# A float32 first stage and TensorE transposes for the first batch of an FFT-and-MLP kernel

## The chip, the cores and the metric

The kernel runs on one core of a Trainium2 chip. The metric is the device time of one execution in microseconds (us). A core has five engines that each work through an instruction list of their own: TensorE (PE, matmuls; its weight loads are PEld), VectorE (DVE), ScalarE (ACT), GpSimd (POOL) and SyncE (SP, which here issues nearly all DMA transfers). Engines wait for one another through semaphores.

## The reference

For each of 8 batches with a sequence of 3136 rows and 256 channels:

```python
y  = irfft(rfft(x, axis=1) * F, n=3136, axis=1)      # F = filt_r + 1j*filt_i, 1569 x 256
u  = y + real(fft(fft(y, axis=1), axis=2))
un = (u - mean(u)) / sqrt(var(u) + 1e-06)            # over the 256 channels
out = u + maximum(un @ w_ch1, 0) @ w_ch2             # 256 -> 1024 -> 256
```

Everything is float32 outside; the products run in float16 on scaled values that are split into a high and a low half.

## The kernel before

**Tiling.** Each transform of length 3136 is two stages of 56-fold matmuls. For one batch, in order:

- `load_x` loads seven tiles `x` of 112x1024 (DMA issue L495) and `measure_x` takes each one's largest magnitude (L387). `weigh_x`, `pow2` and `spread` make a power of two `sx` of it: a TensorE transpose of 1 column (L364), a row maximum (L367), a broadcast (L381) and its copy (L383).
- `first` works on 14 pieces of 112x512: `x16`, the scaled high half (ACT, L533) and low half (DVE, L535); three float16 matmuls (L544); the result is split into `ast` high (ACT, L549) and low (DVE, L551) and stored to DRAM (L554).
- `load_at` loads seven tiles of 112x2048 back in the other order (L577), for batch 0 with the tables `s2`, `i1`, `i2` and `mix` between them (L582 to L591).
- `spectrum`, once per chunk (7) and channel half (2): 16 small matmuls (L618, L619), the products with the filters from PSUM (DVE, L630, L634), their combination into `yt` (POOL, or DVE for the second half of batch 0: L641, L644, L646), the split of `yt` into `y16` (ACT L653, POOL L659 or DVE L656), and a DMA transpose into `z` (L663).
- `fold` prepares the spectra for the transform over channels (`ef`, `eo`).
- `inverse1`: 14 pieces, twelve matmuls on `z` each (L732 to L734), split into `bt` (L741, L743), stored (L746). `load_b2` loads it back (L760); `inverse2` multiplies it (L779), rescales it into `ys` (L792) and stores `dy` (L803, L807).

**Groups.** The rows are then taken in 49 groups of 512: 256 rows of the first half of a sequence and the 256 that mirror them, as two `y` tiles of 128x512. `fetch` loads `y` (L825). `prepare` adds the channel transform: TensorE `mix` (L860), DVE `scaled_add` (L870), one `keep` copy for a batch's first row (ACT, L920), then statistics (L948, L949, L952 to L964). `normalize` makes `un` (L977), splits it into `u16` (L982; L985 or L988) and transposes it by DMA into `ut` (L991). `products` multiplies by the first weight (L1013) and the second (L1054), with `rectify` between them (L1041, L1043). There are 392 product steps, eight a group.

**Weights and filters.** `weight` loads raw words (L1096) and unpacks them on ACT and DVE (L1119 to L1129, L1135); `split_weights` scales and splits them (L1159 to L1163). The filters are loaded as `ft`, measured (`measure_filters`, ACT or POOL squares and DVE L429), and scaled in place by `scale_filters`.

**What sets the order.** The engines' lists are written by a planner (`Plan`). Each function above is a generator that yields an engine and an estimated duration; the planner runs them against a clock of its own, and of the tasks that stand ready for an engine it takes the one with the lowest priority number. Rings (`take`, `give`) count buffers, events (`done`, `until`) are dependences. `gate(t)` holds a task until product step t; a negative t holds nothing and only ranks. So batch 0 comes first, all of its stages have negative numbers, and the later batches are spread under the product steps:

```python
s0 = end - 1.2 - BACKED - 13 * HALF if b else -80
t0 = s0 - 4.6 - 13 * PIECE if b else -100
plan.spawn(load_x(b, t0 - 8.5 if b else -280), t0 - 8.5 if b else -280)
plan.spawn(prepare(g), 8 * g + FIRST)
```

Batch 1's `load_x` also waits until `inverse2` of batch 0 has placed a piece (`until(("placed", 0, 1))`).

## Time and profile before

| | before |
|---|---|
| median of 3 runs | 1521.86 us (1519.93 to 1523.29) |
| profiled execution | 1524.17 us |
| its span in the trace | 1522.4 us, 29999 instructions |
| mean granted TensorE clock | 0.95 |
| PE busy | 1379.6 us (91%) |
| DVE busy | 1114.9 us (73%) |
| ACT busy | 784.4 us (52%) |
| POOL busy | 541.5 us (36%) |
| DMA | 273.12 MB, mean 179 GB/s |

The profile is of one execution. Its span runs from the first instruction to the last; the execution's own time lies 1.8 us over it. A busy share is an average over all stages, so it has to be read stage by stage: with all eight batches in one span, the 91% of TensorE say little of the first 200 us. PEclk is the clock that TensorE was granted, as a share of 2.4 GHz. In the rows, a tile's name stands without its number, `out<-in`.

### The profile page before, as it was taken

Reading aid. Unit: us, or ns where it says so; the run is one execution under the profiler, and the core shown is the slowest. Engines: PE = TensorE matmul, PEld = TensorE weight load, DVE = VectorE, ACT = ScalarE, POOL = GpSimd, SP = SyncE. Lnnn points to the kernel's source line nnn. Section 1 sums busy time; section 2 is a strip of 40 time slices with the busy share of each in tenths; the row PEclk is TensorE's granted clock in tenths of the full one; section 3 lists DMA queues with packets and bytes.
Section 4 is the critical chain, followed back from the end, with each engine's and each line's share of the span. In section 5 each row is a group of like instructions: output and inputs, shape, how many; then the busy total and the mean of one; then the engine's idle time right before and its main releaser. Section 6 shows DMA issues by size and latency. Waiting matters only on the chain.

```text
span 1522.4 us, 29999 instructions
## 1 busy us (share of the span) xinstructions
PE 1379.6 (91%) x11217; PEld 935.0 (61%) x11217; DVE 1114.9 (73%) x2409; ACT 784.4 (52%) x1450; POOL 541.5 (36%) x675
## 2 busy tenths in 40 slices
PE   3442599999999999999999999999999999999998
PEld 1341257765776567666666666666666677666666
DVE  6774977787787877888688867878778878465563
ACT  4543565455464655565555545465455646443442
POOL 4461046501671038400860057211760167210100
PEclk9555589999999999999999999999999999999999
DMA  7999497956988698948987599758997698735521
GB/s 214 207 211 220 126 197 165 241 144 175 220 189 198 170 211 172 263 123 197 226 178 213 144 214 214 218 138 192 210 196 197 163 218 181 179 83 124 132 68 43
DMA packets 419827, 273.12 MB, mean 179 GB/s; under 512 B 234048, under 2 KB 361072, under 8 KB 419680
## 3 DMA queue, kind: packets, MB, share of 16 engines
q1 hardware_dynamic: 419680, 271.19, 77.0%
q8 instruction: 88, 1.44, 0.4%
q14 instruction: 59, 0.48, 0.1%
HBM read 113.31 MB, written 102.76 MB: 142 GB/s over the span
## 4 chain that ended last, share of the span: by engine, by line
PE 56%; DVE 4%; DMA 2%; issue 2%; ACT 1%; SPq 1%; POOL 1%; ACTq 0%; POOLq 0%; DVEq 0%
PE acc L1054 23%; PE h L1013 23%; PE y L779 3%; PE s L544 2%; PE mix L860 2%; DVE y L870 1%; PE i L732 1%; PE i L734 1%; PE i L733 1%; DMA ut<-u 1%; PE s L618 1%; PE s L619 1%; DMA b<-d 1%; DVE st L948 1%; DVE h L1043 1%
## 5 line engine op out<-in xcount | busy, mean ns | idle before, releaser
L1054 PE MATMUL acc<-w2s,h 128*128 128x256 f16 x4704 | 591.9, 273 | 2.8 <-DVE y L1068 2.7
L1013 PE MATMUL h<-ut,w1s 128*128 128x512 f16 x2352 | 578.0, 382 | 16.1 <-DMA ut<-u 11.6
L1054 PEld LDWEIGHTS <-h 128*128 128x128 f16 x4704 | 452.0, 98 | 142.3 <-issue 18.8
L1041 ACT ACTIVATE h<-h 128x512 f16<-128x512 f32 x392 | 233.5, 596 | 482.7 <-PE h L1013 481.9
L1043 DVE SCALAR_TENSOR_TENSOR h<-h,h 128x512 f16<-128x512 f32 x392 | 268.3, 684 | 213.9 <-ACT h L1041 213.1
L1013 PEld LDWEIGHTS <-w1s 128*128 128x128 f16 x2352 | 228.4, 98 | 222.9 <-issue 19.6
L988 POOL TENSOR_TENSOR u<-un,u 128x512 f16<-128x512 f32 x94 | 109.6, 1167 | 598.4 <-ACT u L982 524.6
L870 DVE SCALAR_TENSOR_TENSOR y<-mix,alpha,y 128x508 f32<-128x508 f32 (+1 forms) x368 | 160.5, 475 | 38.6 <-PE mix L860 33.4
L544 PE MATMUL s<-x,s 112*112 112x512 f16 x336 | 100.3, 425 | 20.6 <-ACT x L533 9.7
L644 POOL TENSOR_TENSOR yt<-yt,t 128x224 f32<-128x224 f32 x105 | 70.2, 668 | 134.3 <-DVE yt L636 83.4
L977 ACT ACTIVATE un<-y,sb 128x256 f32<-128x256 f32 x196 | 110.7, 595 | 12.5 <-DVE sb L964 8.5
L659 POOL TENSOR_TENSOR y<-yt,y 128x448 f16<-128x448 f32 x105 | 109.6, 1048 | 18.7 <-ACT y L653 15.4
L630 DVE TENSOR_TENSOR yt<-s,ft 128x448 f32<-128x448 f32 x112 | 69.1, 617 | 32.2 <-PE s L619 29.3
L535 DVE SCALAR_TENSOR_TENSOR x<-x,sx,x 112x512 f16<-112x512 f32 x111 | 86.9, 808 | 6.4 <-ACT x L533 6.3
L732 PE MATMUL i<-z,i 112*112 112x256 f16 x224 | 65.5, 292 | 25.2 <-DMA z<-y 20.1
L551 DVE TENSOR_TENSOR ast<-s,ast 112x512 f16<-112x512 f32 x112 | 74.5, 684 | 15.3 <-ACT ast L549 14.9
L711 POOL TENSOR_TENSOR eo<-ef,eo 128x448 f16<-128x448 f32 (+6 forms) x62 | 59.7, 966 | 71.8 <-ACT eo L708 71.6
L387 DVE TENSOR_REDUCE mx<-x 112x1 f32<-112x1024 f32 x56 | 67.5, 1211 | 23.6 <-DMA x<-x 23.6
L743 DVE TENSOR_TENSOR bt<-i,bt 112x512 f16<-112x512 f32 x112 | 74.8, 684 | 13.6 <-ACT bt L741 13.3
L948 DVE BATCH_NORM_STATS2 st<-y 128x6 f32<-128x256 f32 x196 | 80.8, 412 | 3.0
L792 ACT ACTIVATE ys<-y,alpha 128x512 f32<-128x512 f32 x112 | 73.4, 685 | 18.2 <-PE y L779 18.0
L544 PEld LDWEIGHTS <-s 112*112 112x112 f16 x336 | 46.3, 143 | 56.6 <-issue 37.1
(130 smaller groups left out, 1609.8 us busy)
## 6 DMA issues: line engine op xcount, KB each, us to landing
x<-x SPq DMA_DIRECT2D x56, 448.0 KB
d<-ast SPq DMA_DIRECT2D x112, 224.0 KB
at<-d SPq DMA_DIRECT2D x56, 448.0 KB
d<-bt SPq DMA_DIRECT2D x112, 224.0 KB
b<-d SPq DMA_DIRECT2D x56, 448.0 KB
out<-y SPq DMA_DIRECT2D x98, 256.0 KB
y<-dy SPq DMA_DIRECT2D x92, 256.0 KB
dy<-ys SPq DMA_DIRECT2D x96, 224.0 KB
```

Of the source, the lines that this page charges most:

```text
L535: nc.vector.scalar_tensor_tensor(x16[:, 1], x, sx[:112, 1:2], x16[:, 0], op0=ALU.mult, op1=ALU.subtract)
L544: nc.tensor.matmul(p, s1[:, hs], x16[:, hx], start=i == 0, stop=i == 2)
L659: nc.gpsimd.tensor_tensor(y16[:, :, 1, :112], ytv, y16[:, :, 0, :112], op=ALU.subtract)
L732: nc.tensor.matmul(p[:, i], i1[:, j + i, 0], z[:, i, 0], start=True, stop=False)
L870: nc.vector.scalar_tensor_tensor(out, p, al, y, op0=ALU.mult, op1=ALU.add)
L948: nc.vector.bn_stats(st[:, 2 * t + k], y[:, t, k])
L977: nc.scalar.activation(un[:, k], y[:, t, k], AF.Identity, bias=sb[:, i, 1:2], scale=sb[:, i, 3:4])
L988: nc.gpsimd.tensor_tensor(u16[:, :, :, 1], unv, u16[:, :, :, 0], op=ALU.subtract)
L1013: nc.tensor.matmul(p.rearrange("p (t k q) -> p t k q", t=2, k=2), w1s[:, d, hw, 128 * f : 128 * f + 128], utv[:, :, :, d, hx], start=i == ...
L1041: nc.scalar.activation(h[:, 0], p, AF.Relu)
L1043: nc.vector.scalar_tensor_tensor(h[:, 1], p, 0.0, h[:, 0], op0=ALU.max, op1=ALU.subtract)
L1054: nc.tensor.matmul(acc[:, kind], h[:, hh, c0 : c0 + 128], w2s[:, f, hw], start=f == 0 and kind == 0 and i == 0, stop=f == 7 and kind == 1 ...
```

## The change

Line numbers of the changed kernel are its own.

1. **First stage of batches 0 and 1** (`WIDE = 2`): one float32 matmul per piece on x as it was loaded (L534), with the table `s1f` in float32. The scale `sx` is applied in the eviction (ACT L551, DVE L556), so `x16` falls away. In batch 0 the pieces use four `psf` and two `pso` banks, and `ast` is also kept in buffers of `un`, `u16` and `h`; the first six pieces are multiplied before `sx` is known.
2. **Filters unscaled.** `scale_filters` goes. `conjugate` turns the sign of part of `ft`, and the scale `pF` is a scalar of the filter product (`filtered`, L654), in all batches. Six of the eight filter squares are ACT's, four were.
3. **Batch 0's spectra transposed on TensorE.** `yt` is laid out as [128, 2, 448]; four float32 transposes per chunk and half (L680) go into a `psh` bank, and ACT (L685) and DVE (L687) split that into `z`. The 14 DMA transposes of batch 0 and its `y16` go. Its spectra use the `pso` banks.
4. **Loads.** Tables are issued by `load_tables`, the first two of `s2` ahead of the stores' end. Batch 1's x no longer waits for `placed` and is ranked ahead of batch 0's second inverse. All weights are loaded early, four of them into `w1s` and `w2s` themselves.
5. **Group 0 ahead.** Its channel mixing runs when the last spectrum of batch 0 is done, in `pso` banks; each half has its own `weigh` and is spawned to `normalize` by itself. The first two `b2` and `inverse2` are ranked at -60.

```diff
     def first(b, q, t):
-        yield until(("sx", b), *((("s1",),) if b == 0 else ()))
+        yield until(*((("sx", b), ("s1",)) if b >= WIDE else (("s1f",), ("x", b, q // 2))))
...
+        elif b or q > 5:
+            yield until(("sx", b))
+        kp = yield take(ring)
...
+        if wide:
+            yield "PE", 0.86 if b else 1.2
+            nc.tensor.matmul(p, s1f, x, start=True, stop=True)
...
+            yield until(("sx", b))
...
         yield "ACT", 0.53
-        nc.scalar.copy(st[:, :, 0], p)
+        if wide:
+            nc.scalar.activation(st[:, :, 0], p, AF.Copy, scale=sx[:112, 1:2])
...
         yield "DVE", 0.64
-        nc.vector.tensor_tensor(st[:, :, 1], p, st[:, :, 0], op=ALU.subtract)
+        if wide:
+            nc.vector.scalar_tensor_tensor(st[:, :, 1], p, sx[:112, 1:2], st[:, :, 0], op0=ALU.mult, op1=ALU.subtract)
...
     def load_x(b, t):
-        if b == 1:
-            yield until(("placed", 0, 1))
...
     def spectrum(b, ch, hf, t):
+        def filtered(out, p, f):
+            nc.vector.scalar_tensor_tensor(out, p, pF[:, 1:2], f, op0=ALU.mult, op1=ALU.mult)
+        filtered(t1, p, fr)
...
+        filtered(t2, p, fi)
...
+        if b == 0:
+            kp = yield take("psh")
+            pt = spare(f"yT_{ch}_{hf}")[:112].rearrange("p (j c) -> p j c", j=4)
+            yield "PE", 1.2
+            for j in range(4):
+                nc.tensor.transpose(pt[:, j], yt[:, hf, 112 * j : 112 * j + 112], ident)
...
+            yield "ACT", 0.53
+            nc.scalar.copy(z[:, :, 0], pt)
+            yield "DVE", 0.64
+            nc.vector.tensor_tensor(z[:, :, 1], pt, z[:, :, 0], op=ALU.subtract)
+            give("psh", kp)
...
     def prepare(g):
+        if g == 0:
+            yield until(("spectrum", 0, 6, 0), ("spectrum", 0, 6, 1))
+            kp, pm = yield from mixing()
         yield until(("y", g))
...
+            if g == 0:
+                yield from weigh(slice(2 * t, 2 * t + 2))
+                plan.spawn(normalize(g, t, y, sb, ut), -56 + t)
...
     def weight(i):
-        at = RAW_AFTER[i]
-        yield until(("d1", 0, at) if at < 14 else ("spectrum", 0, (at - 14) // 2, at % 2))
+        yield until(("at", 0, min(i, 6)))
...
-        yield until(*((("weight", i - 1),) if i else ()))
...
-        end = brought(b, 0) - 4
-        s0 = end - 1.2 - BACKED - 13 * HALF if b else -80
-        t0 = s0 - 4.6 - 13 * PIECE if b else -100
-        plan.spawn(load_x(b, t0 - 8.5 if b else -280), t0 - 8.5 if b else -280)
+        x0, t0, s0, piece, half = ((-280, -100, -80, PIECE, HALF), (-30, -7, 9, 0.9, 1.25))[b] if b < 2 else (0,) * 5
...
+        plan.spawn(load_x(b, x0), x0)
...
-        plan.spawn(fetch(g), 8 * g + FIRST - 3)
-        plan.spawn(prepare(g), 8 * g + FIRST)
+        plan.spawn(fetch(g), 8 * g + FIRST - 3 if g else -56)
+        plan.spawn(prepare(g), 8 * g + FIRST if g else -55)
```

The first place is VectorE's list in batch 0's first stage, from the copy of the scale `sx` on. Before:

```order
L383 COPY sx_0_157<-pb_x0_163 128x2
L535 SCALAR_TENSOR_TENSOR x16_0_0_169<-x_0_0_117,sx_0_157,x16_0_0_169 112x512
L535 SCALAR_TENSOR_TENSOR x16_0_1_170<-x_0_0_117,sx_0_157,x16_0_1_170 112x512
L429 TENSOR_REDUCE mF_112<-squares_1_158 128x1
L551 TENSOR_TENSOR ast_0_0_193<-s1_0_0_179,ast_0_0_193 112x2x256
L551 TENSOR_TENSOR ast_0_1_199<-s1_0_1_189,ast_0_1_199 112x2x256
L535 SCALAR_TENSOR_TENSOR x16_0_3_192<-x_0_1_120,sx_0_157,x16_0_3_192 112x512
L429 TENSOR_REDUCE mF_112<-squares_2_166 128x1
L535 SCALAR_TENSOR_TENSOR x16_0_4_198<-x_0_2_121,sx_0_157,x16_0_4_198 112x512
```

After:

```order
L386 COPY sx_0_174<-pb_x0_177 128x2
L556 SCALAR_TENSOR_TENSOR ast_0_0_183<-s1_0_0_134,sx_0_174,ast_0_0_183 112x2x256
L556 SCALAR_TENSOR_TENSOR ast_0_1_184<-s1_0_1_135,sx_0_174,ast_0_1_184 112x2x256
L556 SCALAR_TENSOR_TENSOR ast_0_2_185<-s1_0_2_139,sx_0_174,ast_0_2_185 112x2x256
L556 SCALAR_TENSOR_TENSOR ast_0_3_186<-s1_0_3_140,sx_0_174,ast_0_3_186 112x2x256
```

The splits of `x16` are gone, the evictions `ast` follow one another from the scale on (five more rows like these come next), and the first filter reduction stands behind the ninth of them.

The second place is SP's list while batch 0's spectra are made, from the load of `at_0_4` on. Before:

```order
L577 DMA at_0_4_305<-d1_0_168 112x8x256
L582 DMA s2_82<-c_s2 112x896
L585 DMA i1_83<-c_i1 112x896
L663 DMA_TRANSPOSE z_0_0_445<-y16_1_105 128x8x128
L663 DMA_TRANSPOSE z_0_0_445<-y16_0_104 128x8x128
L577 DMA at_0_5_330<-d1_0_168 112x8x256
L582 DMA s2_82<-c_s2 112x896
L585 DMA i1_83<-c_i1 112x896
L663 DMA_TRANSPOSE z_0_1_493<-y16_2_106 128x8x128
L577 DMA at_0_6_366<-d1_0_168 112x8x256
L582 DMA s2_82<-c_s2 112x896
```

After:

```order
L589 DMA at_0_4_246<-d1_0_133 112x8x256
L596 DMA s2_83<-c_s2 112x896
L600 DMA i1_84<-c_i1 112x896
L596 DMA s2_83<-c_s2 112x896
L600 DMA i1_84<-c_i1 112x896
L596 DMA s2_83<-c_s2 112x896
L600 DMA i1_84<-c_i1 112x896
L603 DMA i2_85<-c_i2 112x512
L605 DMA mix_86<-c_mix 128x640
L1165 DMA w1s_93<-w1 128x1024
L589 DMA at_0_5_262<-d1_0_133 112x8x256
L1165 DMA w1s_93<-w1 128x1024
L589 DMA at_0_6_277<-d1_0_133 112x8x256
```

The transposes into `z` no longer stand between the loads; the tables stand in one run, and two raw weights follow them.

The third place is SP's list around group 0's `y`, from the last stores of `dy` ahead of `b2_0_3` on. Before:

```order
L803 DMA dy_0_1091<-ys_0_1_1074 56x4x256 x2
L760 DMA b2_0_3_1094<-d2_0_116 112x8x256
L495 DMA x_1_0_895<-x 112x1024
L1096 DMA raw_5_1136<-w2 128x1024
L495 DMA x_1_1_896<-x 112x1024
L495 DMA x_1_2_897<-x 112x1024
L495 DMA x_1_3_921<-x 112x1024
L495 DMA x_1_4_956<-x 112x1024
L495 DMA x_1_5_994<-x 112x1024
L825 DMA y_0_118<-dy_0_1091 128x512 x2
L495 DMA x_1_6_1025<-x 112x1024
```

After, from the store of a `bt` in chunk 5 on:

```order
L784 DMA d2_0_116<-bt_0_5_1_971 112x1024
L487 DMA x_1_5_970<-x 112x1024
L487 DMA x_1_6_1041<-x 112x1024
L784 DMA d2_0_116<-bt_0_6_0_1030 112x1024
L784 DMA d2_0_116<-bt_0_6_1_1042 112x1024
L798 DMA b2_0_0_1063<-d2_0_116 112x8x256
L798 DMA b2_0_1_1069<-d2_0_116 112x8x256
L798 DMA b2_0_2_1104<-d2_0_116 112x8x256
L841 DMA dy_0_1119<-ys_0_0_1086 56x3x256
```

The loads of batch 1's x and the raw weights, which stood between the `dy` stores and `y_0`, now stand among the stores of `bt`, ahead of the first load of `b2` (the other tiles of x and the weights further up). After the row `b2_0_3`, `y_0` is next:

```order
L841 DMA dy_0_1119<-ys_0_1_1112 56x4x256
L845 DMA dy_0_1119<-ys_0_0_1086 28x256
L841 DMA dy_0_1119<-ys_0_1_1112 56x4x256
L845 DMA dy_0_1119<-ys_0_0_1086 28x256
L798 DMA b2_0_3_1131<-d2_0_116 112x8x256
L863 DMA y_0_119<-dy_0_1119 128x512 x2
L841 DMA dy_0_1119<-ys_0_2_1157 56x4x256 x2
```

Nothing of batch 1 is left between the `dy` stores and `y_0`.

## Rows read from the trace of the kernel before

**Rows 1.** Busy time by stage: us, then each engine (x instructions), PEclk, DMA share, GB/s
```profile
0.00:20.00 20.00, 0.93 (x3) 0.74 (x4) 9.71 (x15) 2.49 (x5) 2.99 (x12) 1.00 0.92 260
20.00:55.20 35.20, 18.16 (x45) 7.88 (x44) 26.36 (x48) 24.05 (x47) 15.64 (x17) 0.85 0.57 176
55.20:115.00 59.80, 27.84 (x308) 25.43 (x308) 46.83 (x79) 27.58 (x56) 41.56 (x49) 0.56 1.01 214
115.00:152.00 37.00, 8.70 (x55) 4.46 (x55) 16.44 (x26) 13.26 (x24) 4.78 (x4) 0.55 0.91 222
152.00:179.00 27.00, 11.21 (x37) 5.36 (x37) 23.95 (x66) 10.81 (x21) 0.00 (x0) 0.50 0.42 127
179.00:202.60 23.60, 19.98 (x65) 9.00 (x66) 19.52 (x42) 22.23 (x42) 3.46 (x3) 0.64 0.50 144
202.60:1522.40 1319.80, 1292.82 (x10706) 882.13 (x10703) 972.10 (x2136) 684.02 (x1257) 473.09 (x591) 1.00 0.78 177
```

**Rows 2.** Timeline, first stage: start us, us, engine line op, tiles, [idle before <-releaser]
```profile
19.75 0.16 DVE L383 COPY sx<-pb_x 128x2 f32<-128x2 f32 x1 [0.68 <-PE pb_x L381]
...
42.09 0.42 PE L364 MATMUL pt_F<-ident,mF 128*1 128x128 f32 x1
...
48.04 0.68 DVE L551 TENSOR_TENSOR ast<-s,ast 112x512 f16<-112x512 f32 x1
...
51.01 0.32 SPq L577 DMA_DIRECT2D at<-d  x1
...
55.28 0.23 PE L618 MATMUL s<-s,at 112*128 112x56 f16 x1 [8.64 <-DMA at<-d]
```

**Rows 3.** Groups by line and shape, VectorE, 0 to 204 us: busy us, mean ns | idle before
```profile
L535 DVE SCALAR_TENSOR_TENSOR x<-x,sx,x 112x512 f16<-112x512 f32 x27 | 24.3, 918 | 2.0 <-ACT x L533 2.0
L551 DVE TENSOR_TENSOR ast<-s,ast 112x512 f16<-112x512 f32 x28 | 18.6, 685 | 4.3 <-ACT ast L549 4.0
L387 DVE TENSOR_REDUCE mx<-x 112x1 f32<-112x1024 f32 x14 | 17.1, 1220 | 19.4 <-DMA x<-x 19.4
L1121 DVE SCALAR_TENSOR_TENSOR w<-raw,cv 128x512 int32<-128x512 int32 x8 | 6.2, 781 | 0.2
```

**Rows 4.** Groups by line and shape, VectorE, 55 to 115 us
```profile
L743 DVE TENSOR_TENSOR bt<-i,bt 112x512 f16<-112x512 f32 x14 | 9.3, 683 | 3.4 <-ACT bt L741 3.4
...
L630 DVE TENSOR_TENSOR yt<-s,ft 128x448 f32<-128x448 f32 x14 | 8.6, 616 | 5.2 <-PE s L619 4.9
...
L656 DVE TENSOR_TENSOR y<-yt,y 128x448 f16<-128x448 f32 x7 | 5.4, 773 | 0.7 <-ACT y L653 0.7
```

**Rows 5.** Waits, 0 to 240 us: engine line waited for: us, times, longest us
```profile
PE i L732 <- DMA z<-y: 18.3, 3, 7.8
```

**Rows 6.** Timeline, second inverse to dense work, 112 to 206 us
```profile
114.21 0.69 DVE L743 TENSOR_TENSOR bt<-i,bt 112x512 f16<-112x512 f32 x1 [0.59 <-ACT bt L741]
...
123.78 1.92 PE L779 MATMUL y<-b,i 112*64 112x256 f16 x12 [10.27 <-DMA b<-d]
...
133.48 2.59 SPq L495 DMA_DIRECT2D x<-x  x5
...
152.04 0.40 ACT L920 COPY keep<-y 1x256 f32<-1x256 f32 x1 [4.42 <-DMA y<-dy]
...
155.65 1.66 DVE L870 SCALAR_TENSOR_TENSOR y<-mix,alpha,y 128x508 f32<-128x508 f32 x3
...
175.28 0.66 DVE L985 TENSOR_TENSOR u<-un,u 128x512 f16<-128x512 f32 x1
...
179.06 5.30 PE L1013 MATMUL h<-ut,w1s 128*128 128x512 f16 x12 [3.59 <-DMA ut<-u]
...
202.65 2.50 PE L1013 MATMUL h<-ut,w1s 128*128 128x512 f16 x6
```

**Rows 7.** Page, costliest groups of the whole span: busy us, mean ns | idle before
```profile
L1041 ACT ACTIVATE h<-h 128x512 f16<-128x512 f32 x392 | 233.5, 596 | 482.7 <-PE h L1013 481.9
...
L1043 DVE SCALAR_TENSOR_TENSOR h<-h,h 128x512 f16<-128x512 f32 x392 | 268.3, 684 | 213.9 <-ACT h L1041 213.1
```

More of the change, by code (lines that the diff above doesn't have):

```diff
@@ L31 @@
 LAG = 2
+WIDE = 2
 YBUFS = 5
@@ L106, in until, with set @@
         self.post(t, self.resume, task, None)
-    def set(self, event):
-        event.time = self.end
+    def set(self, event, now=False):
+        event.time = self.now if now else self.end
         for task, events in event.waiting:
@@ L537, in first @@
             )
[L538 to L547 removed]
+            if q % 2:
+                give("big", 21 * b + q // 2)
+        elif b or q > 5:
+            yield until(("sx", b))
@@ L904, in prepare, with mixing @@
         yield until(*(("eo", b, c) for b, c in pieces(g, 224)), *((("i2",),) if g == 0 else ()))
+        tiles = [(256 * g + 128 * t, 256 * g + 128 * t + 128) for t in range(2)]
+        ring = "psf" if g else "pso"
+        def mixing():
+            kp = yield take(ring)
+            pm = bank(f"mix_{g}") if g else ps_o.tile([128, 512], F32, tag="pso", name="mix_0")
+            pm = pm.rearrange("p (t c) -> p t c", t=2)
+            for t, (g0, g1) in enumerate(tiles):
+                r0 = g0 % RING
+                yield "PE", 0.4
+                channels(pm[:, t], lambda e, h: eo[:, e, h, r0 : r0 + 128], t == 0, t == 1)
+            mixed[0] = 256 * g + 256
+            done("mixed", g)
+            return kp, pm
+        if g == 0:
+            yield until(("spectrum", 0, 6, 0), ("spectrum", 0, 6, 1))
+            kp, pm = yield from mixing()
         yield until(("y", g))
-        tiles = [(256 * g + 128 * t, 256 * g + 128 * t + 128) for t in range(2)]
         y = ys_of.pop(g)
@@ L921, in prepare, with weigh @@
                     nc.scalar.copy(keep[row, 1], pn)
-                    give("psf", kn)
+                    give(ring, kn)
                     fix = t, row, keep, alphas[b], ku
-        kp = yield take("psf")
-        pm = bank(f"mix_{g}").rearrange("p (t c) -> p t c", t=2)
-        for t, (g0, g1) in enumerate(tiles):
-            r0 = g0 % RING
-            yield "PE", 0.4
-            channels(pm[:, t], lambda e, h: eo[:, e, h, r0 : r0 + 128], t == 0, t == 1)
-        mixed[0] = 256 * g + 256
-        done("mixed", g)
+        if g:
+            kp, pm = yield from mixing()
         mv = tp.tile([128, 4, 2], F32, tag="mv", name=f"mv_{g}")
         st = tp.tile([128, 4, 6], F32, tag="st", name=f"st_{g}")
+        sb = tp.tile([128, 4, 4], F32, tag="sb", name=f"sb_{g}")
+        def weigh(part):
+            yield "ACT", 0.25
+            nc.scalar.activation(sb[:, part, 0], mv[:, part, 1], AF.Sqrt, bias=eps)
+            mu, v = mv[:, part, 0], mv[:, part, 1]
+            r, q, c, s = (sb[:, part, i] for i in range(4))
+            yield "DVE", 0.25
+            nc.vector.reciprocal(r, r)
+            yield "DVE", 0.25
+            nc.vector.scalar_tensor_tensor(q, r, -8.0, r, op0=ALU.mult, op1=ALU.mult)
+            yield "DVE", 0.25
+            nc.vector.scalar_tensor_tensor(c, v, EPS, q, op0=ALU.add, op1=ALU.mult)
+            yield "DVE", 0.25
+            nc.vector.scalar_tensor_tensor(s, c, 24.0, r, op0=ALU.add, op1=ALU.mult)
+            yield "DVE", 0.25
+            nc.vector.scalar_tensor_tensor(q, mu, -1.0, s, op0=ALU.mult, op1=ALU.mult)
+        if g == 0:
+            kt = yield take("ut")
+            ut = mp.tile([128, 2, 8, 128], F16, tag="ut", name=f"ut_{g}", bufs=2)
+            ready[g] = y, ut, kt
         for t, (g0, g1) in enumerate(tiles):
@@ L1097, in weight @@
             done("raw", i)
-            yield until(("raw", i))
+            yield until(("raw", i), *((("weight", i - 2),) if i > 1 else ()))
         ws, m = raws[name]
```

298 lines of the change are left out of this document (155 added, 143 removed).

## The prediction

> **What bounds the kernel now.** I read the busy time by stage first [rows 1]. From 202.6 us to the end TensorE is busy 1292.8 of 1319.8 us at the full clock: nothing but its own work counts there. The 202.6 us ahead of it are different: TensorE is busy 86.8 us of them (the sum of the first six rows), mostly at the lower of its two clock levels (1.2 GHz). This stretch is a chain through one batch, and the kernel ends earlier by what that chain loses. The other batches run under the products, so an edit to them counts only as TensorE time.
>
> The timeline gives the joints of the chain. The scale of x is there at 19.9 us, the last split of the first stage is done at 48.7, the first spectrum starts at 55.3 [rows 2]. The last `bt` is split by 114.9, second inverse matmuls start at 123.8, the first `y` row is touched at 152.0, mixed rows are added from 155.7, and group 0's first product starts at 179.1; dense work starts at 202.65 [rows 6].
>
> The sum is made against the profiled execution, 1524.2 us; the median of the runs is 2.3 us lower, and I take the difference off at the end.
>
> **First stage (0 to 55.3).** Removed: per piece one ACT scaling and one DVE split of 0.92 us [rows 3]; the three float16 matmuls become one float32 matmul on x as loaded, which waits only for x and a PSUM bank. Six banks are open before the scale is known, so six of 14 pieces are multiplied in the idle time ahead of 19.9, and eight remain. No row has a float32 matmul of 512 columns. The nearest is the float32 transpose of 128 columns, 0.42 us [rows 2], so 1.67 us for 512. From above: a matmul that is issued as two such halves, 3.34 us. From below it is free, and VectorE's eviction sets the pace: 14 x 0.69 [rows 3]. I take 1.67, the only row of that type and engine at the same low level: the first bank is free at 21.2 (19.9, then an ACT pass of 0.6 as [rows 7] and a split of 0.69), 8 x 1.67 = 13.4, the last eviction another 1.3: 35.9. (Below: 19.9 + 0.6 + 9.6 = 30.1. Above: 21.2 + 26.7 + 1.3 = 49.2, no gain.) The way from the last split to the first spectrum took 6.6 us; two table loads of 196 KB now lie ahead of it, 1.5 us at the 260 GB/s of the first 20 us to 1.8 at the 214 of the next stage [rows 1], partly beside the last stores; I add 1.0: spectra start at 43.5, **11.8 us** earlier. Filter measuring moves to ACT, six squares instead of four; it ends before the spectra, and its cover is the matmuls' pace: without it, two squares.
>
> **Spectra to the last `bt` (59.6 us now).** The 14 transposing transfers go, and the wait for them: TensorE waited 18.3 us for z [rows 5]. But VectorE is busy 46.8 of 59.8 us and the DMA queues are full, share 1.01 [rows 1].
> - VectorE: the filter product gets a scalar. A three-operand form over 512 PSUM elements takes 684 ns [rows 7], 1.34 ns each; the two-operand form over 448 took 616 [rows 4], 1.38: nothing. Off: seven splits `y` of 0.77 (5.4). Added: 14 splits of the transposed tile, priced as `bt`, 0.68 each (9.6) [rows 4]. Two more weights are unpacked here, four operations of 0.78 at most each [rows 3], 5.8 with the short one, and one maximum of x 1.2. Sum 58.0.
> - ACT loses the filter scaling, and 14 casts of `z` replace 14 of `y`: busy 27.6 of 59.8 us [rows 1], not counted.
> - TensorE: 27.8 us busy now, plus 56 transposes of 0.42 = 23.5: 51.3.
> - DMA, from tile shapes: spectra inputs 3.2 MB, tables 2.9, weights 4.2, `bt` 3.2 and, new here, batch 1's x 3.2: 16.7 MB. At 214 GB/s from about 38 us that ends at 116, with x and the weights at the 260 of the first 20 us [rows 1] at 110.
>
> So three engines each need about what the stage takes today, and I expect no gain in it: `bt` done at 103, second inverse at 114 instead of 123.8 (the 8.9 us between them stay, and 2 for the DMA backlog). Bounds 104 (TensorE's 51.3 alone, then 8.9) and 120 (116 and one load of 4.3, as long as the first input took from its issue [rows 2]).
>
> **`y` of group 0.** It took 28.3 us from the second inverse to its landing, because batch 1's x was issued ahead of it on SP's queue, from 133.5 on [rows 6]. The change puts those loads, and the weights, before the second inverse: six x tiles and one weight, 3.3 MB at 222 GB/s [rows 1] = 14.6 us. Landing at 114 + 13.7 = 127.7. VectorE, which now has six maxima (1.22 [rows 3], 7.3 in all) and four weights (2.9 each, 11.6) between the last `bt` and this add, is free at 103 + 7.3 + 11.6 + about 3 for three scale chains = 125, just ahead. One copy of `keep` later, at 128.5, the add starts (155.7 now).
>
> **Add to first product** took 23.4 us (155.65 to 179.06), with VectorE busy 23.95 of 27 us [rows 1, 6]. The channel mixing is now done ahead and each half normalises by itself, but VectorE's order still puts both halves, two evictions of batch 1 and part of group 1 before the second half's split, so I leave 23.4: first product at 151.9, **27 us** earlier.
>
> **First product to dense work.** Until 202.65 TensorE waited for the second weight matrix. By then three first-product steps, one second-product step and an inverse were done, about 6 us of work at the full clock (half of the 0.44 us that 512 columns took at the lower level [rows 6]): as good as dense from 196.7 with batch 1's first stage done. After: the weights are split before group 0, so dense from 151.9, but six of batch 1's pieces, for which there is no idle time left (0.84 us each at the full clock, half of 1.67), and some 1.5 us of low clock come on top: 158.4. Gain **38.3**.
>
> **Behind that** nothing of the 1319.8 us goes: the filter product's new form and the new tile layout are VectorE, ACT and GpSimd work under TensorE. That cover is 348 us wide for VectorE (972 of 1320 busy). I take 1 us for batch 1's tighter chain and its float32 matmuls. 1524.2 - 37.3 = 1486.9, against the median **1485 us**.
>
> **Rivals.**
> *Less: TensorE sets the spectra's pace.* Its 51.3 us are at the low level. If it still stands in line for the transposes' inputs as it now does for z, 51.3 + 18.3 = 69.6, 10 us over 59.6: 1495; with the float32 matmul at its upper bound instead, 13 more than forecast, 1498; both, 1508. For it: the granted clock was 0.56 in that stage, and the products of one chunk now stand behind another's transposes on one queue. Against: the transposes wait for the same engines as the products do, so their waits may fall into one.
> The Trainium skill, "TensorE: Matmul & The Clock Gate", Part 4 (PE-mode transpose), says that a transpose does not count as busy for the clock. By that rule the added 23.5 us would lift nothing and this rival is the likelier; here 0.56 was granted without any of them, so the trace cannot yet say.
> *More.* The queue waits vanish with the transposing transfers and the bounds from below hold: second inverse at 104 and first stage at 30.1, 10 + 6 us less: 1469. For it: VectorE's rows in that stage are swollen (splits 773 against the 683 of a larger one). Against: the full DMA queues.
> *Slower: batch 1 starves the products.* Ten of its 14 first-stage stores now fall into the dense stretch, 2.3 MB on top of about 20.7 (106 us at 195 GB/s, my estimate between the rows' 177 and 214), before batch 0's groups run out. At the 127 GB/s of 152 to 179 the 23 MB take 181 us, 75 over: 1560. It decides below 23 MB / (106 + 37 us) = 161 GB/s. Against: 127 was a stretch with the queues half idle (0.42), and under demand they moved 214 to 222.
> *No change*: the weights or batch 1's maxima hold group 0 back until 179 after all. VectorE has 22 us of work there, not 52.
>
> **Numbers.** Forecast 0.58 (1475 to 1494), less 0.17, more 0.19, slower 0.04, no change 0.02. The first three are faster: 0.94. A difference of 0.2%, 3 us, is about what a measurement of this kernel can tell. The range leaves out the slower end and the edges: 1464 to 1508; it takes in the bounds of the first stage (-6, +13) and of the second inverse (-10, +6), which need not fall together.
>
> **What would show it.** First spectrum near 43.5 us, with float32 matmuls of 1.7 us; `bt` ending near 103; no x load between `dy` and `y`; first add near 128; first product near 152, and TensorE dense from there. I am wrong if the dense stretch, from its first product on, shows waits on DMA of more than a few us, if the transposes take far from 0.42 us, or if the first product comes later than 165.

## The result and the profile after

The changed kernel takes 1481.88 us (median) against 1522.57 us: a ratio of 0.972, 95% interval 0.968 to 0.976. It was timed a second time beside the last experiments: 1483.14 us, ratio 0.9752 (0.9738 to 0.9765). The forecast was 1485, the range 1464 to 1508. One of the changed kernel's first four runs took 2082.58 us, at a granted clock of 0.648, and is not in the ratios.

| | before | after |
|---|---|---|
| median of 4 runs | 1522.57 us | 1481.88 us |
| profiled execution, its span | 1524.17, 1522.4 us | 1478.77, 1477.0 us |
| mean granted TensorE clock | 0.95 | 0.966 |
| PE busy | 1379.6 us | 1379.7 us |
| DVE, ACT, POOL busy | 1114.9, 784.4, 541.5 us | 1109.6, 763.7, 528.5 us |
| DMA | 273.12 MB | 269.48 MB |

The median before has one run more than the three ahead of the prediction, 1528.86 us. TensorE is busy for the same 1380 us. What went is its idle time, 142.8 us before and 97.3 after. First the busy time by stage, with the stages cut at nearly the same joints as in [rows 1] (118.0 is the first add and not the touch of `y` 0.6 us before it; the last two lines are the product stretch, cut once more at 165 us):

```profile
0.00:18.30 18.30, 8.40 (x15) 3.33 (x15) 9.67 (x15) 3.94 (x7) 1.28 (x10) 0.95 0.91 277
18.30:39.10 20.80, 9.34 (x19) 3.69 (x19) 11.76 (x29) 12.84 (x27) 6.96 (x10) 0.75 0.91 291
39.10:97.40 58.30, 36.66 (x380) 32.51 (x380) 53.75 (x96) 24.28 (x46) 38.00 (x42) 0.70 0.92 261
97.40:118.00 20.60, 8.32 (x40) 4.43 (x41) 19.19 (x47) 13.66 (x29) 3.72 (x3) 0.50 0.67 187
118.00:142.00 24.00, 14.80 (x43) 5.48 (x41) 22.95 (x63) 16.45 (x30) 6.73 (x6) 0.64 0.39 106
142.00:165.00 23.00, 23.00 (x138) 12.89 (x137) 13.86 (x25) 11.65 (x20) 0.00 (x0) 0.98 0.67 181
165.00:1477.00 1312.00, 1279.19 (x10615) 872.08 (x10613) 978.43 (x2122) 680.85 (x1251) 471.84 (x590) 0.99 0.73 177
```

The six lines up to 165 us answer to the first six of [rows 1]: 165 us in place of 202.6, with more product work done in them. In the spectra's stage, from 39.1 to 97.4 us, VectorE is busy 53.8 us for 46.8, TensorE 36.7 for 27.8, and the DMA queues moved 261 GB/s where they moved 214. TensorE's granted clock is 0.70 there, it was 0.56.

The joints of the chain, from the timeline:

```profile
18.19 0.16 DVE L386 COPY sx<-pb_x 128x2 f32<-128x2 f32 x1 [0.68 <-PE pb_x L384]
...
20.11 8.70 PE L534 MATMUL s<-x,s1f 112*112 112x512 f32 x16 [1.95 <-DVE ast L556]
...
31.07 0.75 DVE L556 SCALAR_TENSOR_TENSOR ast<-s,sx,ast 112x512 f16<-112x512 f32 x1 [0.42 <-ACT ast L551]
...
39.16 0.23 PE L635 MATMUL s<-s,at 112*128 112x56 f16 x1 [5.49 <-DMA at<-d]
...
43.64 1.94 PE L680 MATMUL yT<-ident,yt 128*112 128x128 f32 x8
...
96.78 0.68 DVE L781 TENSOR_TENSOR bt<-i,bt 112x512 f16<-112x512 f32 x1
...
104.19 3.62 PE L817 MATMUL y<-b,i 112*64 112x256 f16 x20 [1.29 <-DMA b<-d]
...
117.42 0.40 ACT L981 COPY keep<-y 1x256 f32<-1x256 f32 x1
...
117.97 1.79 DVE L912 SCALAR_TENSOR_TENSOR y<-mix,alpha,y 128x508 f32<-128x508 f32 x4
...
140.90 3.69 PE L1080 MATMUL h<-ut,w1s 128*128 128x512 f16 x12
...
148.60 0.82 PE L1121 MATMUL acc<-w2s,h 128*128 128x256 f16 x6
```

Against [rows 2] and [rows 6]: the scale of x comes 1.6 us earlier, the last split of the first stage ends at 31.8 us for 48.7, the first spectrum starts at 39.2 for 55.3, the last split of `bt` at 96.8 for 114.2, the second inverse at 104.2 for 123.8, `y` is touched at 117.4 for 152.0, the first add at 118.0 for 155.7, the first product at 140.9 for 179.1. The second product now follows 7.7 us behind the first; it stood at 200.1 before.

Behind that there is something new. The two longest waits of the product stretch, from the timeline of TensorE:

```profile
316.78 3.73 PE L543 MATMUL s<-x,s 112*112 112x512 f16 x8 [8.41 <-DVE x L522]
...
818.48 2.58 PE L543 MATMUL s<-x,s 112*112 112x512 f16 x5 [5.62 <-DVE x L522]
```

TensorE stood 8.4 us at 308 us and 5.6 us at 813, at two seams between batches. The kernel before had no wait over 2.8 us behind 202.6 us. Both came again in the second profile of the changed kernel, 8.38 and 5.61 us: they are in the lists, not in the run.

### The profile page after: what moved, and what is told of

Same layout as the page of the kernel before. It is cut to its first block, busy times and chain, and to the rows that moved or that the text cites. A ratio compares the mean times of both kernels' runs of the same rounds, so it can differ in the third digit from the quotient of the medians.

```text
span 1477.0 us, 29967 instructions
## 1 busy us (share of the span) xinstructions
PE 1379.7 (93%) x11245; PEld 934.4 (63%) x11245; DVE 1109.6 (75%) x2391; ACT 763.7 (52%) x1407; POOL 528.5 (36%) x660
## 2 busy tenths in 40 slices
DMA packets 405297, 269.48 MB, mean 182 GB/s; under 512 B 219408, under 2 KB 346656, under 8 KB 405152
## 4 chain that ended last, share of the span: by engine, by line
PE 50%; DVE 6%; DMA 1%; ACT 1%; issue 0%; POOL 0%; SPq 0%; ACTq 0%; DVEq 0%
PE acc L1121 20%; PE h L1080 20%; PE y L817 2%; DVE y L912 2%; PE s L543 2%; PE mix L902 1%; DVE h L1110 1%; DVE st L1025 1%; PE i L770 1%; DMA ut<-u 1%; PE s L635 1%; PE i L772 1%; PE i L771 1%; PE s L636 1%; DVE y L1135 1%
## 5 line engine op out<-in xcount | busy, mean ns | idle before, releaser
L1080 PEld LDWEIGHTS <-w1s 128*128 128x128 f16 x2352 | 227.9, 98 | 210.5 <-issue 12.7
L668 POOL TENSOR_TENSOR yt<-yt,t 128x224 f32<-128x224 f32 x98 | 64.5, 658 | 159.9 <-DVE t L654 157.0
L697 POOL TENSOR_TENSOR y<-yt,y 128x448 f16<-128x448 f32 x98 | 100.7, 1034 | 7.5 <-ACT y L695 7.0
L654 DVE SCALAR_TENSOR_TENSOR yt<-s,pF,ft 128x448 f32<-128x448 f32 x98 | 66.4, 677 | 31.2 <-PE s L636 29.2
L654 DVE SCALAR_TENSOR_TENSOR t<-s,pF,ft 128x448 f32<-128x448 f32 x126 | 84.1, 674 | 6.6 <-PE s L636 6.6
L779 ACT CAST bt<-i 112x512 f16<-112x512 f32 x112 | 65.2, 586 | 33.9 <-PE i L772 26.0
L543 PE MATMUL s<-x,s 112*112 112x512 f16 x252 | 67.4, 392 | 16.1 <-DVE x L522 14.8
L830 ACT ACTIVATE ys<-y,alpha 128x512 f32<-128x512 f32 x112 | 73.5, 685 | 11.9 <-PE y L817 11.6
L1135 DVE SCALAR_TENSOR_TENSOR y<-acc,beta,y 128x512 f32<-128x512 f32 x98 | 70.5, 742 | 11.8 <-PE acc L1121 11.3
L390 DVE TENSOR_REDUCE mx<-x 112x1 f32<-112x1024 f32 x56 | 67.0, 1209 | 10.1 <-DMA x<-x 10.1
L720 POOL TENSOR_TENSOR ef<-yt 128x224 f32<-128x224 f32 x112 | 72.9, 671 | 0.8 <-DVE yt L665 0.4
```

Of the source, the lines that this page charges most:

```text
L543: nc.tensor.matmul(p, s1[:, hs], x16[:, hx], start=i == 0, stop=i == 2)
L654: nc.vector.scalar_tensor_tensor(out, p, pF[:, 1:2], f, op0=ALU.mult, op1=ALU.mult)
L697: nc.gpsimd.tensor_tensor(y16v[:, 1], yh, y16v[:, 0], op=ALU.subtract)
L1080: nc.tensor.matmul(p.rearrange("p (t k q) -> p t k q", t=2, k=2), w1s[:, d, hw, 128 * f : 128 * f + 128], utv[:, :, :, d, hx], start=i == ...
L1135: nc.vector.scalar_tensor_tensor(y[:, t], acc, beta, y[:, t], op0=ALU.mult, op1=ALU.add)
```

## Experiments

Twelve runs followed, one of them of the changed kernel itself (after_again). The table gives the joints of each profiled execution in us from the span's start (the last `bt` is the start of its split). "Rest" is the span less the start of the first second-product. The two executions of the changed kernel differ by 1.4 to 2.6 us at every joint from the scale of x on (18.2 and 19.9), so a head's difference under 2.5 us says nothing. "Against changed" is against the mean of its two medians, 1482.5. The kernel before took 1519.17 to 1522.57 us beside the several groups of runs, and the changed one lay 40.7 and 37.1 us under it, so under 4 us that column says nothing by itself. The ratios given below are to the kernel before, beside the run.

| kernel | median | against changed | first spectrum | last `bt` | second inverse | first add | first product | first second-product | rest |
|---|---|---|---|---|---|---|---|---|---|
| before | 1522.57 | +40.1 | 55.3 | 114.2 | 123.8 | 155.7 | 179.1 | 200.1 | 1322.3 |
| changed | 1481.88 | | 39.2 | 96.8 | 104.2 | 118.0 | 140.9 | 148.6 | 1328.4 |
| after_again | 1483.14 | | 41.4 | 98.3 | 105.6 | 119.5 | 143.0 | 151.2 | 1329.3 |
| dma_transposes | 1496.01 | +13.5 | 40.5 | 101.6 | 120.6 | 136.8 | 154.8 | 164.1 | 1332.8 |
| narrow | 1498.26 | +15.8 | 52.1 | 108.7 | 115.9 | 131.8 | 155.1 | 163.2 | 1334.4 |
| group0_plain | 1493.30 | +10.8 | 39.9 | 97.0 | 104.7 | 126.1 | 143.5 | 152.6 | 1339.8 |
| weights_late | 1500.82 | +18.3 | 43.2 | 97.7 | 107.5 | 130.2 | 148.1 | 167.8 | 1331.0 |
| before_x1_free | 1519.00 | +36.5 | 55.8 | 112.2 | 125.3 | 147.7 | 168.8 | 194.1 | 1322.7 |
| twice_pe | 1489.59 | +7.1 | 40.2 | 102.9 | 111.1 | 128.7 | 147.3 | 156.5 | 1330.2 |
| twice_dve | 1487.13 | +4.6 | 41.7 | 97.9 | 106.2 | 123.1 | 144.7 | 154.5 | 1331.1 |
| wide1 | 1487.22 | +4.7 | 40.4 | 97.1 | 104.5 | 120.2 | 143.5 | 152.0 | 1331.7 |
| b1_sooner | 1478.69 | -3.8 | 41.0 | 98.0 | 105.5 | 119.4 | 143.2 | 150.1 | 1327.8 |
| b1_denser | 1489.07 | +6.6 | 42.6 | 99.7 | 107.1 | 120.9 | 144.7 | 151.6 | 1334.7 |
| come16_sooner | 1466.65 | -15.9 | 39.9 | 97.0 | 104.5 | 118.4 | 142.1 | 149.8 | 1315.0 |

Every kernel has three first-product steps behind it when the rest begins. "before" and "before_x1_free" also have the whole of batch 1's first stage behind them, the changed kernel ten of its 14 pieces, so the rest of these two is not to be compared with the others: four pieces at 0.86 us are 3.4 us.

### One part undone at a time

**dma_transposes.** In `spectrum`, with the low half of `y16` on VectorE again for the second channel half of batch 0:

```diff
-        if b == 0:
+        if b < 0:
             kp = yield take("psh")
...
-        yield "POOL", 1.03
-        nc.gpsimd.tensor_tensor(y16v[:, 1], yh, y16v[:, 0], op=ALU.subtract)
+        if b == 0 and hf == 1:
+            yield "DVE", 0.55
+            nc.vector.tensor_tensor(y16v[:, 1], yh, y16v[:, 0], op=ALU.subtract)
...
```

> The changed kernel with batch 0's spectra transposed by DMA again (14 transposing transfers, y16 split), all else as changed. My theory, from the prediction's sum (three engines each need what the stage takes, so the transposes alone exchange one cost for another): within 4 us of the changed kernel's 1481, that is 1477 to 1485, and the stretch from the first spectrum to the last split of bt stays near the 58.2 us of the changed kernel. Rival (the wait for z set that stage, and TensorE's transposes removed it): 10 to 18 us slower, 1491 to 1499, the stretch 68 us or longer, with TensorE waiting for z on DMA again.

Measured: 1496.01 us, ratio 0.9834 (0.9809 to 0.9860). The rival had the time right, 13.5 us, and mostly the wrong place. TensorE does wait for `z` on DMA again, 13.7 us in four waits, but the stage grew by less: 61.1 us from the first spectrum to the start of the last `bt` split for 57.6. Most of the loss stands behind it: 19.0 us from there to the second inverse, 7.4 in the changed kernel. Busy time by stage of that stretch, SP's issues in it, and TensorE's first second-inverse matmul:

```profile
97.00:121.00 24.00, 5.03 (x22) 4.04 (x24) 21.32 (x42) 11.31 (x24) 2.31 (x2) 0.50 1.03 289
...
102.81 4.94 SPq L487 DMA_DIRECT2D x<-x  x5
...
110.21 0.93 SPq L802 DMA_DIRECT2D b<-d  x2
...
120.64 3.62 PE L821 MATMUL y<-b,i 112*64 112x256 f16 x20 [2.26 <-DMA b<-d]
```

The DMA queues are full (1.03) and move 289 GB/s: five loads of batch 1's x are now issued behind the last split of `bt`, and weights shortly ahead of it, all in front of the loads of `b2`; in the changed kernel the last x was issued by 94.8 us, ahead of that split. The same stretch of the changed kernel is short and its queues are not full (0.62):

```profile
97.40:104.20 6.80, 0.38 (x3) 0.12 (x3) 6.63 (x13) 3.07 (x9) 0.00 (x0) 0.50 0.62 173
```

So the transposes on TensorE paid, and less by the wait for z of [rows 5] than by the loads that are now early. With the transposing transfers the queues moved 203 GB/s at a share of 1.24 between 60 and 70 us, without them 363 at 1.07. Whether this queue time or the transposes' places in SP's list held the loads back is not separated.

**narrow.**

```diff
-WIDE = 2
+WIDE = 0
...
-        yield "SP", 0.3, -60
+        yield "SP", 0.3, -300
         nc.sync.dma_start(s1, a["c_s1"])
```

> The changed kernel with WIDE = 0: the first stage of batches 0 and 1 in three float16 matmuls on scaled and split x again, its table loaded first; all else as changed. My theory (the float32 first stage brought the first spectrum forward by most of the 16.1 us between 55.3 and 39.2, and the chain behind it passes that on whole): first spectrum at 50 to 54, time 11 to 15 us over the changed kernel's 1481: 1492 to 1496. Rival (the chain behind absorbs it, since weights and batch 1's maxima hold group 0 anyway): less than 5 us slower.

Measured: 1498.26 us, ratio 0.9847 (0.9823 to 0.9871), first spectrum at 52.1 us. This is my theory, with a time 2.3 us over its range: the 11.8 us that the first spectrum lost against the mean of 40.3 are still there at the first product (13.2). Nothing behind it took them up.

**group0_plain.** `prepare(0)` takes the path of every other group, at its old ranks:

```diff
...
-        plan.spawn(fetch(g), 8 * g + FIRST - 3 if g else -56)
-        plan.spawn(prepare(g), 8 * g + FIRST if g else -55)
+        plan.spawn(fetch(g), 8 * g + FIRST - 3)
+        plan.spawn(prepare(g), 8 * g + FIRST)
```

> The changed kernel with group 0 prepared as every other group (mixing after y has come, one chain for both halves, its old ranks). My theory (the prediction left 23.4 us from add to first product, and the trace after shows 22.9, so preparing ahead gives little): within 4 us of the changed kernel's 1481. Rival (it is what keeps the 22.9 from growing, because batch 1's evictions would come in between): 8 us or more slower.

Measured: 1493.30 us, ratio 0.9817 (0.9795 to 0.9838). My theory misses. The rival has the time (10.8 us), but not its reason. The first add comes 7.4 us later, but the first product only 1.6 and the first second-product 2.7 us later than the mean of the changed kernel's two. So the 22.9 us from add to product did not grow; they shrank to 17.5. The rest, where the edit changes no work, is 10.9 us longer. TensorE's busy time behind 160 us says where, here and in the second execution of the changed kernel:

```profile
160.00:1492.40 1332.40, 1295.67 (x10685) 882.07 (x10683) 991.39 (x2135) 683.97 (x1255) 471.93 (x590) 0.99 0.73 175
```

```profile
160.00:1480.50 1320.50, 1286.74 (x10675) 877.15 (x10672) 983.28 (x2134) 682.79 (x1254) 471.30 (x590) 0.99 0.74 177
```

TensorE is idle 36.7 us here and 33.8 there, and busy 1295.7 for 1286.7 us with nearly the same instructions. Of these 9 us about 5 are a lower clock behind more, shorter waits (my estimate from the granted clock in steps of 10 us: eight steps lie under 0.97, four in after_again). An edit in the head gives the planner another order for everything behind it, and that order is worth some us by itself.

**weights_late.** The weights at their old places and buffers, one after another:

```diff
-RAW_IN = (None, None, "ys", "ys", "ut", "ut", None, None)
+RAW_IN = ("ys", "ys", "b2", "ut", "ut", "ys", "b2", "ys")
+RAW_AFTER = (6, 7, 8, 9, 10, 17, 18, 15)
...
-            yield until(("raw", i), *((("weight", i - 2),) if i > 1 else ()))
+            yield until(("raw", i))
```

> The changed kernel with the weights loaded and unpacked one after another at their old places (as in the kernel before). My theory (the early weights are what lets the second product follow the first: 11 us of the prediction's sum, and what kept the early x alone from paying in the kernel before): first product within 5 us of 140.9, first second-product 15 us or more after it, time 10 to 16 us over the changed kernel's 1481: 1491 to 1497. Rival (VectorE has room for them): under 4 us slower.

Measured: 1500.82 us, ratio 0.9870 (0.9833 to 0.9908): 18.3 us, more than I expected, and the largest of the four. The first product and the first second-product on TensorE:

```profile
148.08 5.30 PE L1081 MATMUL h<-ut,w1s 128*128 128x512 f16 x12 [21.31 <-DMA ut<-u]
...
167.76 0.37 PE L1122 MATMUL acc<-w2s,h 128*128 128x256 f16 x1 [1.65 <-ACT w2s L1234]
```

The second product stands 19.7 us behind the first, as the theory has it (21 us before, 7.7 changed); the first product is also 6 us late, which the theory did not have. The four parts undone cost 58.4 us together, more than the whole change gained, so their prices cannot be added.

**before_x1_free.** The kernel before with

```diff
-        if b == 1:
-            yield until(("placed", 0, 1))
```

> The kernel before with one thing changed: batch 1's x no longer waits until a piece of the second inverse is placed, so its loads stand among the stores of bt and not ahead of group 0's y. My theory (those loads held y back by 14.6 us): from the first second-inverse matmul to the first touch of y 14 to 17 us instead of 28.3; first product 9 to 15 us earlier than 179.1; time 1508 to 1514 against 1522.6. Rival (the second weight matrix and VectorE's list hold the products anyway): under 4 us faster.

Measured: 1519.00 us against 1520.73 for the kernel before, ratio 0.9980 (0.9962 to 0.9998): the rival. Half of the mechanism was right: from the second inverse to the first touch of `y` it took 19.6 us for 28.3, and the first product came 10.2 us earlier. But TensorE's next row is the end of that gain:

```profile
168.84 4.15 PE L1011 MATMUL h<-ut,w1s 128*128 128x512 f16 x12
...
194.10 0.37 PE L1052 MATMUL acc<-w2s,h 128*128 128x256 f16 x1 [1.65 <-ACT w2s L1159]
```

The second product waits for the second weight matrix until 194.1 us, 6.0 earlier than before. Early x alone is worth 0.2%; with the weights early beside it, taking those away costs 18.3 us. Weights early without x was not run.

### What sets the spectra's stage

**twice_pe.** Each transpose twice (`for j in (0, 1, 2, 3, 0, 1, 2, 3)`).

> The changed kernel with each of the 56 transposes of batch 0 made twice into the same bank: 56 x 0.24 = 13.4 us more of TensorE between the first spectrum and the last split of bt, nothing more for any other engine. My theory (VectorE, busy 53.8 of 58.3 us there, sets that stage): the stage under 62 us, time within 4 us of 1481. Rival (TensorE's queue sets its pace): the stage 68 us or longer, time 1489 to 1495.

**twice_dve.** Each low half of `z` twice:

```diff
             nc.vector.tensor_tensor(z[:, :, 1], pt, z[:, :, 0], op=ALU.subtract)
+            nc.vector.tensor_tensor(z[:, :, 1], pt, z[:, :, 0], op=ALU.subtract)
```

> The changed kernel with each of the 14 low halves of the transposed tile made twice on VectorE: 14 x 0.68 = 9.5 us more of VectorE in the same stage, nothing more for any other engine. My theory (VectorE sets that stage): the stage 65 us or longer, time 6 to 10 us over 1481: 1487 to 1491. Rival (its 4.5 idle us and the waits of others take it): the stage under 61 us, time within 3 us of 1481.

Measured: 1489.59 us (0.9793, 0.9755 to 0.9831) and 1487.13 us (0.9776, 0.9731 to 0.9821). The second interval takes in the changed kernel's own ratios, so its 4.6 us are not clear of the noise.

The doubled transposes cost TensorE less than the 13.4 us that I had expected. Busy time on the line of the transposes, from 30 to 110 us, in the changed kernel and with each made twice:

```profile
30.00:110.00 80.00, 11.86 (x56) 8.04 (x56) 0.67 0.86 243
```

```profile
30.00:110.00 80.00, 19.20 (x112) 16.28 (x112) 0.75 0.78 229
```

That is 7.3 us more. The stage to the end of the last `bt` split took 63.4 us for 58.3 and 57.5, and the time grew by 7.1: nearly all of it came through. My theory, with under 62 us and under 4 us, is wrong; the rival has the time, and a stage shorter than its 68 us.

twice_dve does not decide about the stage. The last `bt` was no later than in the changed kernel's two executions, because the planner moved unpacking of weights behind it (5.5 us of it are left in the stage, 12.6 were there), and the first add came 4.4 us later. So the stretch in which VectorE's time can be judged ends at the first add and not at `bt`: from 39.1 to 118 us of the changed kernel VectorE is busy 72.9 of 78.9 us.

The stage's own 58 us are a chain through several engines, as far as the waits tell. TensorE waits there 7.7 us in seven waits for GpSimd's `yt`, ahead of the transposes, 6.3 for loads of `at`, and at the end 2.9 us for the last low half of `z`, ahead of which VectorE's list has the unpacking of a weight:

```profile
91.93 0.37 PE L771 MATMUL i<-z,i 112*112 112x256 f16 x1 [2.93 <-DVE z L687]
```

No run slows or relieves GpSimd, which is busy 38.0 of the 58.3 us; its part is untested.

### Batch 1 and the rest

**b1_sooner.** `(-30, -7, 9, 0.9, 1.25)` becomes `(-30, -7, 6, 0.9, 1.25)`.

> The changed kernel with batch 1's spectra and what follows them ranked three product steps earlier (s0 6 for 9, as near as the kernel before had it, 5.15); the mixing of group 6, the first with rows of batch 1, comes at step 41 of TensorE's list for 46. My theory (the 8.4 us in which TensorE stands at 308 us are batch 1's y coming too late for group 6, because that chain was given less time; the part of the sum that I put at 1 us): that wait is gone or under 2.5 us, time 8 to 11 us under the changed kernel's 1481: 1470 to 1474. Rival (the wait is VectorE's order at the seam of two batches, whenever the chain starts): the wait stays over 6 us, time 1478 to 1485.

**b1_denser.** It becomes `(-30, -7, 8, 0.9, 1.05)`.

> The changed kernel with batch 1's spectra one product step earlier and 1.05 steps apart for 1.25 (s0 8, half 1.05), so that they end 3.6 steps earlier while they start almost as now. My theory (its y must only come sooner for group 6; starting sooner cost the first product 2.3 us in the run that began three steps earlier): no wait over 2.5 us near 308, first product within 1 us of 140.9, time 1472 to 1478. Rival (the idle time of the dense stretch only moves elsewhere, as it did there): 1478 to 1483.

Measured: 1478.69 us (0.9720, 0.9683 to 0.9758) and 1489.07 us (0.9792, 0.9777 to 0.9807). In both, the wait at 308 us is gone. That does not yet show its cause, since it is also gone or small in runs that leave batch 1's ranks alone. What it goes with in all of them is the product step at which TensorE mixes group 6, the first group with rows of batch 1. At step 46 (the changed kernel twice, twice_dve) the wait is 8.4 us. At step 45 (dma_transposes, weights_late, twice_pe) there are three or four waits of at most 1.4 us. At 41 or 42 (the two runs here, come16_sooner, narrow, wide1, group0_plain) there is none at that place. So the wait goes with group 6 being prepared late, as my theory has it. The wait itself is in VectorE's list, as the rival has it: VectorE works through it, with the adds and statistics of group 7 ahead of the split of x that TensorE's next matmul needs.

```profile
309.63 1.79 DVE L912 SCALAR_TENSOR_TENSOR y<-mix,alpha,y 128x508 f32<-128x508 f32 x4
...
312.54 1.75 DVE L912 SCALAR_TENSOR_TENSOR y<-mix,alpha,y 128x508 f32<-128x508 f32 x4
...
315.99 0.74 DVE L522 SCALAR_TENSOR_TENSOR x<-x,sx,x 112x512 f16<-112x512 f32 x1
```

The time did not follow. b1_sooner's ratio is that of the changed kernel (0.972 and 0.9752) within the noise, and b1_denser lost 6.6 us: the rest is 1327.8 and 1334.7 us where the changed kernel has 1328.4 and 1329.3, because other waits opened later (3.2 us at 534 and 4.2 at 1315 in the one, 2.8 at 707 in the other, where the 5.6 near 820 stayed too). The expected times failed twice here, though the wait went as expected.

**wide1.** `WIDE = 1`.

> The changed kernel with batch 1's first stage in three float16 matmuls on split x again, batch 0's in float32. My theory (VectorE, busy 23.0 of 24.0 us from group 0's first add to its first product, is relieved by not splitting x: 14 x 0.72 = 10 us, a part of it in that stretch): first product 3 to 7 us later than 140.9, time 1484 to 1489. Rival (a float32 matmul costs TensorE 0.87 us a piece against about 0.65 at the full clock, and this is the 1 us that I put on batch 1): first product within 1 us, time 1478 to 1481.

Measured: 1487.22 us, ratio 0.9783 (0.9769 to 0.9796), the time of my theory, 4.7 us. But the first product came only 1.6 us later than the mean, less than the two executions of one kernel differ, and not 3 to 7. Which part of the 4.7 is VectorE's relief and which the order behind stays open.

**come16_sooner.** b1_sooner, and `COME = 16` for 15, so that every second inverse is ranked one product step earlier.

> The changed kernel with batch 1's spectra three steps earlier (s0 6) and every later batch's second inverse one product step earlier (COME 16). My theory (each wait of the dense stretch is a batch's y that comes late for its first group): fewer waits over 1 us behind the first product, time 1468 to 1475. Rival (those waits come from the lists' order elsewhere, and earlier inverses only fill the buffers): 1476 to 1486.

Measured: 1466.65 us (1465.37 to 1470.72), ratio 0.9647 (0.9631 to 0.9663): faster than both kernels, by 15.9 us against the changed one, and 1.4 us under my range. Its head is that of the changed kernel (first product at 142.1); the gain lies in the rest. Its busy time behind 160 us and the longest group of TensorE's waits there:

```profile
160.00:1464.80 1304.80, 1283.14 (x10652) 876.33 (x10649) 979.31 (x2129) 682.70 (x1254) 472.14 (x590) 0.99 0.75 179
...
PE h L1080 <- DMA ut<-u: 11.3, 4, 4.9
```

TensorE is idle 21.7 us behind 160 us for 33.8 in after_again, and the two long waits are gone; the longest left is 4.9. That agrees with the theory that a batch's `y` comes late for its first group, but COME alone was not run, and any such number also reorders the lists.

**after_again.**

> The changed kernel once more, unedited, beside the next three on one chip. Expected at 1479 to 1484; how its dense stretch loses time (8.4 us at 308, 5.6 at 813) should repeat within a microsecond if those waits are its list's and not the run's.

It came out as expected: 1483.14 us, both waits as before.

## Why the prediction was right, and which terms were not

The median moved by 40.7 us, and the forecast was 37.3. In the profiled executions it is 45.4 (41.9 in the second), so the sum is within a fifth, but not each of its terms. The head gained 38.2 us to the first product where I had 27.2, and the part behind it 2.9 less than I had. By the prediction's own steps, with the profiled execution after:

| step | forecast gain | measured |
|---|---|---|
| to the first spectrum | 11.8 | 16.1 |
| spectra to the last `bt` | 0 | 1.3 |
| last `bt` to second inverse | -2 | 2.2 |
| second inverse to first touch of `y` | 14.6 | 15.0 |
| to the first add | 2.8 | 3.1 |
| add to first product | 0 | 0.5 |
| first product to the end | 10.1 | 7.2 |

**First stage: the mechanism right, the price too high.** Eight pieces took 8.7 us of TensorE from 20.1 us on, 1.09 each, not 1.67. A piece stands in the trace as two records. Behind the scale the first four records start 0.85 to 0.98 us apart, about 1.7 a piece, and from 23.5 us on the others start 0.43 apart, 0.86 a piece, at a granted clock of 0.82 for the whole: two pieces ran at the lower level and six at the upper. Later rows agree: at a granted clock of 0.50 two pieces took 3.8 us (from 137.3), at 1.00 a piece took 0.86 between products (from 149.3). So my step "8 x 1.67" took the lower level for all eight, from one row at 42.1 us with a granted 0.50 around it, though the old stage as a whole had 0.85 [rows 1]. That 1.67 fits the lower level is luck: 0.42 us is the whole length of a transpose's record, and in a run such records start 0.21 apart at that level, while a piece needs two records of 0.86. The evictions then set the pace, 14 from 19.3 to 31.8 us or 0.89 apart, and of their two engines it was ScalarE, busy 11.9 of the 12.7 us from 19.2 on with filter squares and the sign changes of `conjugate` between them; VectorE waited 3.1 us for it in five waits. The prediction had that in its remark that without the matmuls' pace for a cover two squares count. The scale also came 1.6 us earlier; in after_again it did not (19.9), and there the first spectrum is 13.9 us earlier.

**The spectra's stage: right in sum, by wrong terms.** I expected no gain and there was 1.3 us. But the argument was that three engines each need what the stage takes, and all three figures were too high: VectorE was busy 53.8 us for 58.0, TensorE 36.7 for 51.3, and the queues, which I had busy until 110 to 116 us, were down to a share of 0.62 from 97.4 on. That the stage came out as forecast is therefore luck in part. The largest miss is the transposes: 11.9 us for 23.5. Eight of them took 1.94 us at a granted clock of 0.50, 0.24 each: each record is 0.42 us long, but they start 0.21 us apart. That the transposes take "far from 0.42 us" was one of the prediction's signs of being wrong, and it came. And the filter product's new form was put at nothing; it takes 671 ns for 616:

```profile
L654 DVE SCALAR_TENSOR_TENSOR t<-s,pF,ft 128x448 f32<-128x448 f32 x28 | 17.9, 671 | 6.6 <-PE s L636 6.6
...
L687 DVE TENSOR_TENSOR z<-yT,z 112x512 f16<-112x512 f32 x14 | 9.4, 677 | 1.2 <-ACT z L685 1.2
```

By the means that is 1.5 us over the stage's 28 products, by busy time 0.7 (17.2 before, as two groups of 14). The split of the transposed tile took 677 ns, as priced (0.68).

**DMA.** This step failed: I kept the full queues of [rows 1] and added 2 us behind the stage. The queues moved 261 GB/s instead of 214, and 6.7 us lie between the last split and the second inverse instead of 10.9. dma_transposes shows what it hangs on: with the transposing transfers back, the same loads end later, and the second inverse is 15.8 us later than the mean. I had counted those transfers as a wait of TensorE and not as something that holds up other loads.

**`y` of group 0, its add, its first product**: 13.2 us for 13.7, 0.6 for 0.8, 22.9 for 23.4. before_x1_free and weights_late show that early x alone is worth little, and much with the weights early.

**Behind the first product.** "I take 1 us for batch 1's tighter chain" is the term that failed. TensorE was idle 27.0 us behind 202.6 us [rows 1] and is idle 32.8 us behind 165 now, and one wait of 8.4 us is new. In kind that is the rival "batch 1 starves the products", at about a ninth of its price: batch 1's first group was prepared late, once. The DMA queues were not the reason; between 160 and 300 us they moved 197 GB/s in the mean at a share of 0.81, above the 161 at which I said that it decides. But the wait is not the price either: eight orders without it have a rest within 1 us of the changed kernel's or longer, and only come16_sooner's is shorter.

**The rival "Less"** was weighed with the Trainium skill's page "TensorE: Matmul & The Clock Gate", Part 4, by which a transpose does not count as busy for the clock in the same way. The runs speak against it for these float32 transposes. The 58 us from the first spectrum on, without a transpose of batch 0's spectra on TensorE (dma_transposes), with 56 (the changed kernel) and with 112 (twice_pe):

```profile
40.48:98.48 58.00, 29.14 (x319) 26.46 (x320) 51.20 (x84) 21.59 (x43) 42.26 (x49) 0.59 1.07 235
```

```profile
39.16:97.16 58.00, 36.66 (x380) 32.51 (x380) 53.51 (x95) 24.04 (x46) 38.00 (x42) 0.71 0.92 261
```

```profile
40.19:98.19 58.00, 38.50 (x425) 36.11 (x426) 54.16 (x97) 23.91 (x47) 40.11 (x42) 0.82 0.81 235
```

TensorE's other matmuls there number 319, 324 and 313. The granted clock over these 58 us was 0.56, 0.59 and 0.59 in the three profiles without such transposes, 0.62 to 0.71 in the ten with 56, and 0.82 in the one with 112. In what order the other matmuls fall differs too, so the size of the effect is not shown; its sign holds over all fourteen.

## What to carry to other kernels

Price a new operation from rows at both clock levels, and by the distance between starts in a run of equal ones; a single row's length can be twice that. Where two edits free the same joint (here x and the weights ahead of group 0), look for what ends last after the first of them before giving it a price: alone it can be worth almost nothing. And in a kernel whose lists come from a planner, an edit at the head reorders all that follows: compare kernels by joints, head and rest apart, before a few us are put down to the edit.
